# Forming the third expert's weights at half the pace while the filter stage still runs

## The chip, the cores and the metric

One core of one Trainium2 chip runs the kernel. The metric is the device time of one execution in microseconds (us), the median over the timed runs. One further execution was taken with the hardware profiler; all rows in this document come from it.

The core has a matrix engine (PE, with PEld for its weight loads), a vector engine (DVE), a scalar engine (ACT), GpSimd (POOL) and a queue engine that issues DMAs (SP). Each engine works through its own instructions in the order in which the program lists them.

## The reference

The input is a batch of 4 sequences of 3584 rows with 192 columns, 14336 rows in all. Three things are computed one after the other:

```python
# 1: a causal filter of 7 taps per head (8 heads of 24 columns), softmax-normalised taps
out = einsum('hk,bskhg->bshg', softmax(weight), unfold(x_pad))
# 2: a first mixture of 8 experts, one expert per row, with a skip gate and a residual
compute = x @ w_skip > 0
e = argmax(x @ w_gate); g = max(softmax(x @ w_gate))
x[compute] = x + g * (relu(x @ w1[e]) @ w2[e])
# 3: a second mixture of 8 experts, one per row, no residual
e = argmax(x @ w_gate2 + modality_bias[modality_id])
y = g2 * (relu(x @ w1_2[e]) @ w2_2[e])
```

Every expert has w1 of 192 x 1024 and w2 of 1024 x 192 in float32. The kernel multiplies in 16 bits: each operand is split into a high and a low half, and a product is made of three partial products.

## The kernel before

**Filter stage.** `Phase1.run` (lines 970 to 1003) goes through 128 tiles of 112 rows in 8 groups of 16 tiles. A schedule step `v` filters one head of a group, turns earlier rows round and computes gate logits. `Phase1.fin` (line 934) ends a group: it writes each row's expert number, its "code", into `code`, sets `codes = g + 1` and stores the rows in DRAM. `NG` is 8, so `codes == NG` says that all codes are there.

**Routing.** `Moe.route_a` (line 418) turns the codes of a group into positions: a one-hot table `oha`, a running sum on DVE (the scan that writes `cuma`), two small matmuls of `cuma` with `tri` and `ones`, positions `posa`, `sla`, `qa`, comparison tables `oa` and `ob`, and 16 matmuls of `ob` with `oa` that count. After four groups the rows for the first jobs are known; the groups after that are routed beside those jobs.

**Expert weights.** `Moe.prep` (lines 298 to 406) forms the 16-bit weights of the experts one after the other. It loads w1 and w2 into the tiles `ws`, sums their squares for a scale `wsc`, waits for a free buffer (`guard`), and then forms the high halves on ACT (four copies) and the low halves on DVE (eight instructions of the kind "scalar, tensor, tensor": four for w1, 128x512 each, and four for w2, 128x384 each). Between these pieces it yields `p` (lines 372 to 393), so that one piece is issued every `p` schedule steps. `p` is asked for once per expert, when its forming begins:

```python
            p = pace()
            ...
            lo(o1[:, 1, h:], wt[:, h:], sc[:, 0:1], o1[:, 0, h:])
            yield p
```

When an expert is done, `keep` (line 408) stores its formed weights in DRAM. The load of the next expert's tiles is issued between the pieces too, into buffers that the pieces free.

**Jobs.** `Ffn.run` (line 1181) handles blocks of 128 gathered rows, here called jobs, numbered from 0. A job is two halves of `mm1` (20 matmuls `xt,w1b` each), each followed by a high half `hh` on ACT and a low half `hlo` on DVE, and then 24 matmuls `mm2` (`w2b` with `hh` and `hlo`), which come one job later, and the residual sum `x2a` on DVE. Jobs 0 to 2 use the first expert, 3 to 5 the second, 6 to 8 the third, 9 to 11 the fourth. The buffers of `xt` are three; a DMA transposition on SP fills one.

**The order of the work.** Nothing is scheduled by cost. The generators above are advanced by "ticks" (`Tasks.tick`, line 101): the filter loop ticks twice a step, and the job loop ticks once in each of four places of a job (`bg`, line 1469). The last filter steps (from 76 on) and the first two jobs are interleaved. `late()` (line 1342) is true as soon as the third pair of weight buffers exists, which is when the first jobs begin to be prepared. The third expert begins to be formed at filter step 71, in both kernels; at that point six of eight codes exist. `class InOrder` keeps each engine's instructions in the order in which the generators issued them; DMAs on SP are placed by the framework.

Line 73 is the helper that issues every instruction, so it appears in nearly every row; the tiles' names tell the instructions apart. Those that the text speaks of are `w1b` and `w2b` from `ws` and `wsc` (weights being formed), `cuma<-cont,oha` (the scan), `hh`, `hlo`, `x2a`, and `rA`, `rC` (the start of the second routing, `ranks`, line 530, with its own two matmuls on PE).

Of the kernel before, what the change touches and what calls it, by code (L numbers as in the profile page):

```python
# [28 lines left out]
NG = NT // GT  # L29
# [8 lines left out]
LANES = [(0, e) for e in range(E)], [(1, r) for r in range(NSEL)]  # L38
# [1265 lines left out]
def build(tc, x, cw, m1w1, m1w2, mod, bias2, m2w1, m2w2, wgs, out):  # L1304
    with ExitStack() as ctx:
        m = Moe(tc, ctx)
# [9 lines left out]
        pw = ctx.enter_context(tc.tile_pool(name="pw", bufs=2))  # L1316
        pq = ctx.enter_context(tc.tile_pool(name="pq", bufs=4))
# [3 lines left out]
        p1 = Phase1(m, st, sx, x, rows)  # L1321
# [11 lines left out]
        ws = (m1w1, m1w2, s1[0], s2[0]), (m2w1, m2w2, s1[1], s2[1])  # L1333
        d1, d2 = set(), set()
# [7 lines left out]
        owner, conv, late = [None], [False], lambda: len(ffn.w1b) > 2  # L1342

        def lane(k):
            def guard(q, e):
                if q == 0:
                    return e < 2 or late() and (e < 3 or step[0] >= last(e - 3) + 2)
                if "o" in w and owner[0] in (None, k):
                    owner[0] = k
                    return True  # L1350
                return False

            while k and m.sel is None:
                yield 1
            for t in m.prep(ws, w["pw2"] if k else pw, pq, dst, guard, (d1, d2), LANES[k], k, lambda: 8 if k else 8 if late() else 14, lambda: 1 if late() else 3, owner, conv, 8 if k else 26, lambda: not late(), tkw):
                yield t

        def routes():
# [16 lines left out]
        tk, tk2, tkw = Tasks(), Tasks(), Tasks()  # L1375
# [3 lines left out]
        def phase1():  # L1379
            v = next(gp, None)  # L1380
            if v == 1:
                nc.sync.dma_start(rows[0:128, :], m.dz.bitcast(I32))
                nc.sync.dma_start(rows2[0:128, :], m.dz.bitcast(I32))
            if v == 2:
                tkw.add(lane(0))
            if routed[0] < p1.codes:
                tk.add(m.route_a(routed[0], m.code[:, 0, :], rt, ob, ra))
                routed[0] += 1
            return v
# [15 lines left out]
        w = {}  # L1405

        def late_pools():
            st.close()
            m.py.append(m.py2)
            m.ph.append(m.ph3)  # L1410
            px = ctx.enter_context(tc.tile_pool(name="px", bufs=1))
            w["x"] = px.tile([128, NC - XA, D], F32, name="x2s")
            po = ctx.enter_context(tc.tile_pool(name="po", bufs=1))
            pw2 = sp.enter_context(tc.tile_pool(name="pw2", bufs=2))
            w["pw2"] = pw2
            tkw.add(lane(1))
            o = po.tile([128, 4, F], F16, name="o1"), po.tile([128, W2C + 2], F16, name="o2")
            w["o"] = o
            tk.add(routes())
# [174 lines left out]
```

## Time and profile before

| what | value |
|---|---|
| median of 3 timed runs | 985.49 us (984.07 to 986.93) |
| the profiled execution, its own time | 987.25 us |
| span of that execution, first to last instruction | 985.4 us |
| PE busy | 913.1 us, 93% |
| PEld busy | 851.5 us, 86% |
| DVE busy | 589.1 us, 60% |
| ACT busy | 474.5 us, 48% |
| POOL busy | 511.6 us, 52% |
| mean granted clock of PE | 0.968 |

The profiled execution lies 1.76 us above the median, and 1.85 us of its own time lie outside the span. Busy shares are means over stages with different limits; what limits a stage is read from that stage alone. The granted clock is 1 at 2.4 GHz and 0.5 at 1.2 GHz.

### The profile page before, as it was taken

The numbers are of one execution on the slowest core, as the hardware profiler recorded it, in microseconds if no ns is written. First come the engines' busy times: TensorE is split into PE (matmuls) and PEld (weight loads), VectorE is DVE, ScalarE is ACT, GpSimd is POOL, SyncE is SP. The second block draws the span as 40 slices with busy tenths as digits, with TensorE's granted clock in tenths as the row PEclk, the third lists the DMA queues.
The fourth block names the chain that finished last, engine by engine and source line by source line (L and its number), as shares of the span: only waits on it lengthen the run. The fifth ranks groups of instructions, "written<-read, shape, count | busy, mean of one in ns | idle before, by whom it ended". The sixth has DMA issues, their size and how long they took to land. (4 is left out here: it accounts for less than half of the span.)

```text
span 985.4 us, 28847 instructions
## 1 busy us (share of the span) xinstructions
PE 913.1 (93%) x11000; PEld 851.5 (86%) x11000; DVE 589.1 (60%) x1628; ACT 474.5 (48%) x895; POOL 511.6 (52%) x985
## 2 busy tenths in 40 slices
PE   6999859997999999999899999999999999999993
PEld 4676558997999999988888988999989999999992
DVE  5789977899889887446456465864333333333330
ACT  4877743545676655345545654333333333333330
POOL 5055543733547445575667675554555545555431
PEclk9999857999999999999999999999999999999997
DMA  9595576663949685789534334322552332333240
GB/s 320 207 332 188 188 197 192 177 162 71 299 143 262 200 269 149 244 242 344 140 95 109 98 96 114 72 62 65 144 143 72 72 68 75 74 74 74 71 125 15
DMA packets 105910, 148.96 MB, mean 151 GB/s; under 512 B 80559, under 2 KB 85657, under 8 KB 100640
## 3 DMA queue, kind: packets, MB, share of 16 engines
q1 hardware_dynamic: 91136, 117.50, 38.6%
q0 software_dynamic: 13920, 28.87, 12.8%
q8 instruction: 89, 1.46, 0.6%
q14 instruction: 61, 0.50, 0.2%
q10 hardware_dynamic: 704, 0.63, 0.2%
HBM read 174.22 MB, written 51.08 MB: 229 GB/s over the span
## 5 line engine op out<-in xcount | busy, mean ns | idle before, releaser
L73 PEld LDWEIGHTS <-w1b 128*128 128x128 f16 x4200 | 313.8, 99 | 33.5 <-issue 15.8
L73 DVE SCALAR_TENSOR_TENSOR ws<-bank,ws 128x512 f16<-128x512 f32 x220 | 151.3, 690 | 256.3 <-ACT ws L73 212.0
L73 PEld LDWEIGHTS <-ws 128*128 128x128 f16 (+2 forms) x2696 | 224.0, 98 | 2.6
L73 POOL DMA_INDIRECT out_dram<-u,si x114 | 115.6, 1014 | 183.0 <-ACT u L73 72.3
L73 PE MATMUL bank<-xp,w1b 128*128 128x256 f16 x1680 | 201.7, 274 | 4.4 <-DMA xp<-gt 2.7
L73 PE MATMUL bank<-w2b,ws 128*128 128x192 f16 x2016 | 182.8, 247 | 0.0
L73 ACT ACTIVATE ws<-bank 128x512 f16<-128x512 f32 x220 | 130.4, 597 | 94.2 <-PE bank L73 82.6
L73 PE MATMUL bank<-xt,w1b 128*128 128x128 f16 x2520 | 159.0, 223 | 9.2 <-DVE hlo L73 7.5
L73 ACT ACTIVATE hh<-bank 128x512 f16<-128x512 f32 x132 | 78.4, 594 | 143.5 <-PE bank L73 129.8
L73 ACT ACTIVATE u<-bank,c 128x192 f32<-128x192 f32 x114 | 48.0, 421 | 181.3 <-PE bank L73 156.7
L73 PE MATMUL bank<-w2b,hh 128*128 128x192 f16 x1008 | 134.8, 250 | 0.0
L73 PE MATMUL bank<-w2b,hlo 128*128 128x192 f16 x504 | 126.1, 250 | 0.6 <-DVE hlo L73 0.6
L73 DVE SCALAR_TENSOR_TENSOR hlo<-bank,hh 128x512 f16<-128x512 f32 x132 | 90.1, 686 | 53.8 <-ACT hh L73 47.7
L73 PEld LDWEIGHTS <-hh 128*128 128x128 f16 x1056 | 96.1, 100 | 0.6 <-issue 0.3
L73 POOL DMA_INDIRECT gt<-rows,idxm x62 | 62.5, 1009 | 10.5 <-issue 6.2
L73 POOL TENSOR_TENSOR xs<-gt 128x128 f32<-128x128 f16 x124 | 52.5, 445 | 28.1 <-DVE x2a L73 13.0
L73 PEld LDWEIGHTS <-o 128*128 128x128 f16 x640 | 57.0, 98 | 7.0 <-issue 1.6
L73 PE MATMUL bank<-xp,o 128*128 128x256 f16 x520 | 62.0, 273 | 0.3 <-issue 0.3
L73 POOL DMA_INDIRECT gt<-rows,idx x58 | 57.3, 989 | 9.4 <-issue 7.5
L73 PE MATMUL bank<-xg,band 128*112 128x384 f32 x128 | 57.2, 534 | 1.7 <-DVE hl L73 1.7
L73 PE MATMUL bank<-o,ws 128*128 128x192 f16 x624 | 56.4, 247 | 0.0
L73 ACT COPY xtb<-bank 128x672 f16<-128x672 f16 x64 | 45.9, 719 | 18.7 <-PE bank L73 18.4
(301 smaller groups left out, 1257.7 us busy)
## 6 DMA issues: line engine op xcount, KB each, us to landing
w1b<-s1b SPq DMA_DIRECT2D x45, 1024.0 KB
w2b<-s2b SPq DMA_DIRECT2D x45, 768.5 KB
o<-s1b SPq DMA_DIRECT2D x14, 1024.0 KB
o<-s2b SPq DMA_DIRECT2D x14, 768.5 KB
xg<-in_x_dram SPq DMA_DIRECT2D x7, 1536.0 KB
rows<-hl SPq DMA_DIRECT2D x7, 1386.0 KB
ws<-in_moe_w_dram SPq DMA_DIRECT2D x12, 768.0 KB
s1a<-w1b SPq DMA_DIRECT2D x8, 1024.0 KB
```

Of the source, the lines that this page charges most:

```text
L73: r = f(*args, **kw)
```

## The change

The rate of pieces while `late()` holds was 1 for every expert. It becomes 2 as long as a group's codes are missing. The rate is asked for once per expert, and the third expert is the only one that begins while `late()` holds and codes are missing.

```diff
-            for t in m.prep(..., lambda: 8 if k else 8 if late() else 14, lambda: 1 if late() else 3, owner, conv, ...):
+            for t in m.prep(..., lambda: 8 if k else 8 if late() else 14, lambda: (1 if p1.codes == NG else 2) if late() else 3, owner, conv, ...):
```

The third expert's forming begins at filter step 71 in both kernels; it ends in job 0 before, at the end of job 1 now. What follows it in the same generator moves along: the fourth expert's forming runs from the end of job 4 to the end of job 6 before, from the end of job 6 to the end of job 8 now. The scale of the fifth expert is issued two jobs later, and its forming begins at the same place in both kernels. No instruction is added or removed; the lists of PE, DVE and ACT are the same but for their order, POOL's is unchanged.

DVE, in filter steps 73 to 75, where the sixth group is routed (`oa`) and the seventh group's codes are made (`cd` to `code`); `ws_1363` and `ws_1696` are the third expert's w1 and w2:

```order
 L73 SCALAR_TENSOR_TENSOR code<-codeA,code 128x16
-L73 SCALAR_TENSOR_TENSOR w2b_2047<-ws_1696,wsc,w2b_2047 128x2x192
 L73 TENSOR_REDUCE cd<-gec 112x16
 L73 TENSOR_REDUCE gsm<-gex 112x16
 L73 TENSOR_TENSOR oa<-iq,qa 128x1024
-L73 SCALAR_TENSOR_TENSOR w2b_2047<-ws_1696,wsc,w2b_2047 128x2x192
+L73 SCALAR_TENSOR_TENSOR w1b_2046<-ws_1363,wsc,w1b_2046 128x512
 L73 TENSOR_SCALAR gsm<-gsm 112x16
 L73 RECIPROCAL gt<-gsm 112x16
-L73 SCALAR_TENSOR_TENSOR w2b_2047<-ws_1696,wsc,w2b_2047 128x2x192
 L73 TENSOR_TENSOR code<-pm,cd 112x16
 L73 TENSOR_TENSOR code<-cd,code 112x16
```

Three pieces stood here, and one stands here now.

DVE, a little further on, beside job 0, up to the scan of the seventh group (`ws_1572` is the last part of the third expert's w1):

```order
 L73 SCALAR_TENSOR_TENSOR w2b_2047<-ws_1696,wsc,w2b_2047 128x2x192
 L73 TENSOR_REDUCE L<-bank_62 112x68
-L73 SCALAR_TENSOR_TENSOR w1b_2046<-ws_1572,wsc,w1b_2046 128x512
 L73 SCALAR_TENSOR_TENSOR hlo<-bank_58,hh 128x512
 L73 TENSOR_TENSOR oa<-iq,qa 128x1024
 L73 TENSOR_SCALAR pm<-L 112x16
 L73 TENSOR_TENSOR oha<-code,c_144 128x128
-L73 SCALAR_TENSOR_TENSOR w1b_2046<-ws_1572,wsc,w1b_2046 128x512
+L73 SCALAR_TENSOR_TENSOR w2b_2047<-ws_1696,wsc,w2b_2047 128x2x192
 L73 SCALAR_TENSOR_TENSOR cuma<-cont,oha 128x128
```

All eight pieces stood ahead of this scan, and four do now; of the other four, three now stand between it and the eighth group's scan and one behind that.

DVE, at the end of job 8 and the start of job 9 (`bank_58` in the last row is job 9's first half, `ws_2314` the last part of the fourth expert's w1):

```order
 L73 COPY po<-bank_61 128x2x8
 L73 TENSOR_TENSOR off<-po 128x16
 L73 TENSOR_TENSOR off<-off,gend 128x8
+L73 SCALAR_TENSOR_TENSOR w1b_77<-ws_2314,wsc,w1b_77 128x512
 L73 SCALAR_TENSOR_TENSOR x2a<-bank_64,c,xs 128x192
 L73 SCALAR_TENSOR_TENSOR key<-off,c_144 128x8
-L73 TENSOR_TENSOR gt_3236<-key 128x64
-L73 SCALAR_TENSOR_TENSOR hlo<-bank_58,hh 128x512
-L73 TENSOR_REDUCE key<-gt_3236 128x8
+L73 TENSOR_TENSOR gt_3228<-key 128x64
+L73 SCALAR_TENSOR_TENSOR w1b_77<-ws_2314,wsc,w1b_77 128x512
+L73 SCALAR_TENSOR_TENSOR hlo<-bank_58,hh 128x512
```

The fourth expert's eight pieces, which stood from job 5 to job 7, now all stand behind the second scan of `rC`, and the last of them directly ahead of the first `hlo` of job 9, the first job that uses these weights.

## Rows read from the trace of the kernel before

**Rows 1.** Stretches: length; PE, PEld, DVE, ACT, POOL busy; clock; DMA share; GB/s.

```profile
144.35:158.07 13.72, 11.37 (x124) 11.17 (x124) 11.07 (x37) 6.36 (x13) 5.59 (x13) 0.74 0.87 299
158.07:164.25 6.18, 6.18 (x44) 5.93 (x45) 2.06 (x4) 0.00 (x0) 3.27 (x9) 0.52 1.02 201
164.25:193.75 29.50, 28.48 (x410) 28.30 (x408) 25.54 (x64) 12.69 (x19) 16.67 (x38) 0.98 0.49 141
193.75:211.00 17.25, 17.25 (x264) 17.25 (x262) 15.74 (x62) 10.03 (x21) 6.47 (x16) 1.00 0.95 199
211.00:243.80 32.80, 24.72 (x368) 24.01 (x367) 31.70 (x96) 14.11 (x23) 12.76 (x29) 1.00 0.27 64
243.80:250.00 6.20, 6.20 (x71) 6.03 (x70) 6.17 (x13) 2.86 (x4) 1.27 (x4) 0.74 0.94 340
250.00:400.00 150.00, 150.00 (x2166) 150.00 (x2164) 124.88 (x273) 94.32 (x176) 81.97 (x184) 1.00 0.75 218
...
190.09:197.10 7.01, 6.91 (x102) 6.91 (x103) 5.10 (x19) 4.08 (x8) 5.72 (x15) 1.00 1.04 273
```

**Rows 2.** PE in order of time: start us, us, instruction, count, [idle before, releaser].

```profile
144.35 0.59 PE L73 MATMUL bank<-cuma,tri 128*128 128x8 f32 x2 [5.76 <-DVE cuma L73]
...
146.95 4.45 PE L73 MATMUL bank<-xt,w1b 128*128 128x128 f16 x40
...
158.07 0.39 PE L73 MATMUL bank<-cuma,tri 128*128 128x8 f32 x2 [2.35 <-DVE cuma L73]
...
164.25 2.83 PE L73 MATMUL bank<-xt,w1b 128*128 128x128 f16 x40
```

**Rows 3.** DVE in order of time, 133 to 158 us.

```profile
133.37 0.75 DVE L73 SCALAR_TENSOR_TENSOR w1b<-ws,wsc,w1b 128x512 f16<-128x512 f32 x1 [0.57 <-ACT w1b L73]
...
143.88 0.41 DVE L73 TENSOR_TENSOR_SCAN cuma<-cont,oha 128x128 f32<-128x128 f32 x1
...
147.16 0.22 DVE L73 TENSOR_SCALAR t1a<-bank 128x56 f32<-128x56 f32 x1 [0.76 <-PE bank L73]
...
149.92 0.69 DVE L73 SCALAR_TENSOR_TENSOR hlo<-bank,hh 128x512 f16<-128x512 f32 x1 [1.10 <-ACT hh L73]
...
152.06 0.69 DVE L73 SCALAR_TENSOR_TENSOR hlo<-bank,hh 128x512 f16<-128x512 f32 x1 [0.34 <-ACT hh L73]
...
157.38 0.64 DVE L73 TENSOR_TENSOR_SCAN cuma<-cont,oha 128x128 f32<-128x128 f32 x1
```

**Rows 4.** Groups of DVE instructions, 133.3 to 143.95 us: busy us, mean ns, idle.

```profile
L73 DVE SCALAR_TENSOR_TENSOR w1b<-ws,wsc,w1b 128x512 f16<-128x512 f32 x4 | 3.0, 742 | 0.6 <-ACT w1b L73 0.6
L73 DVE SCALAR_TENSOR_TENSOR w2b<-ws,wsc,w2b 128x384 f16<-128x384 f32 x4 | 2.5, 633 | 0.0
```

**Rows 5.** The same groups on DVE, 177.8 to 188.2 us, the fourth expert.

```profile
L73 DVE SCALAR_TENSOR_TENSOR w1b<-ws,wsc,w1b 128x512 f16<-128x512 f32 x4 | 3.4, 848 | 0.0
...
L73 DVE SCALAR_TENSOR_TENSOR w2b<-ws,wsc,w2b 128x384 f16<-128x384 f32 x4 | 2.6, 649 | 0.0
```

**Rows 6.** DVE in order of time: an `hlo` each of jobs 7, 9 and 12.

```profile
188.27 0.68 DVE L73 SCALAR_TENSOR_TENSOR hlo<-bank,hh 128x512 f16<-128x512 f32 x1
...
197.10 0.69 DVE L73 SCALAR_TENSOR_TENSOR hlo<-bank,hh 128x512 f16<-128x512 f32 x1
...
212.99 0.69 DVE L73 SCALAR_TENSOR_TENSOR hlo<-bank,hh 128x512 f16<-128x512 f32 x1
```

**Rows 7.** PE in order of time: the rC matmul, jobs 9, 12, 13 and 18.

```profile
190.19 0.39 PE L73 MATMUL bank<-rC,tri 128*128 128x8 f32 x2 [1.02 <-DVE rC L73]
...
193.75 2.40 PE L73 MATMUL bank<-xt,w1b 128*128 128x128 f16 x40
...
206.78 2.40 PE L73 MATMUL bank<-xt,w1b 128*128 128x128 f16 x40
...
242.49 1.28 PE L73 MATMUL bank<-xt,w1b 128*128 128x128 f16 x20 [3.93 <-DVE hlo L73]
```

**Rows 8.** SP in order of time: the transpositions of jobs 13 and 14.

```profile
203.10 3.16 SPq L1035 DMA_TRANSPOSE xt<-gt  x2
```

More of the change, by code (lines that the diff above doesn't have):

```diff
@@ L1354, in lane @@
                 yield 1
-            for t in m.prep(ws, w["pw2"] if k else pw, pq, dst, guard, (d1, d2), LANES[k], k, lambda: 8 if k else 8 if late() else 14, lambda: 1 if late() else 3, owner, conv, 8 if k else 26, lambda: not late(), tkw):
+            for t in m.prep(ws, w["pw2"] if k else pw, pq, dst, guard, (d1, d2), LANES[k], k, lambda: 8 if k else 8 if late() else 14, lambda: (1 if p1.codes == NG else 2) if late() else 3, owner, conv, 8 if k else 26, lambda: not late(), tkw):
                 yield t
```

## The prediction

> **What bounds the kernel now.** I read the table by stretches first, then the order of time on PE and DVE around the stretches where PE is not busy throughout. From 250 us on, where the last change of order has long passed, PE is busy all of 150 us [rows 1], so whatever the change does earlier is carried to the end as a shift. Ahead of that, three stretches matter. From 144.35 to 158.07 PE is busy 11.4 of 13.7 us and DVE 11.1, at a mean granted clock of 0.74 [rows 1]. PE waits there twice for the scan that writes `cuma`: 5.76 us ahead of 144.35 and 2.35 us ahead of 158.07 [rows 2]. The scan is late because DVE works through its list with hardly a gap, and the third expert's eight pieces are part of that list, 3.0 and 2.5 us busy [rows 4]. The reader should see that DVE sets the pace here, through two scans. From 164.25 to 211.00 PE is full but for one us and DVE has some slack [rows 1]. From 211.00 to 243.80 it turns round: DVE is busy 31.7 of 32.8 us while PE is busy 24.7 [rows 1], and PE's last long wait, 3.93 us for an `hlo` of job 18, ends at 242.49 [rows 7]. So DVE's backlog when it enters that stretch, in jobs 9 to 12, counts one for one.
>
> The change touches both: it relieves DVE ahead of the first scan, and pushes the fourth expert's pieces toward the second backlog.
>
> **Term A, the scans.** Ahead of the first scan stand two w1 and two w2 pieces fewer: 2 x 0.74 + 2 x 0.63 = 2.75 us by their means [rows 4]. Instructions overlap by about 0.08 us each, so 2.4 us of DVE's time. The first piece also waited 0.57 us for its high half on ACT [rows 3]; now the position arithmetic stands ahead of it and covers that. The first scan comes 2.4 + 0.57, about 2.9 us, earlier, and PE's wait of 5.76 shrinks to 2.9 [rows 2]. ACT and POOL follow: the copies that POOL makes from `gt` wait for the same DVE list, and come about 1.5 us earlier.
>
> Between the two scans three pieces are added, two of w2 and one of w1, 2 x 0.55 + 0.66 = 1.8 us without the overlap. DVE waited there 0.76, 1.10 and 0.34 us, 2.2 us in all [rows 3]. Walking down the list with these durations, the whole 0.76 and some 0.4 of the 1.10 are filled; the rest stays, since the high half `hh` comes from PE at the lower clock and is no earlier relative to the scan. So 1.8 - 1.2 = 0.6 us of the 2.9 are given back, and the second scan comes 2.3 us earlier. The eighth piece stands behind it, where DVE waits for PE anyway (busy 2.1 of 6.2 us [rows 1]). Job 3 starts 2.3 us ahead of its 164.25 [rows 2]. Bounds: 1.1 us if none of the waits is filled (2.9 - 1.8), 2.9 if they cover all. I take 2.3, from the walk.
>
> **Term B, the fourth expert.** Its eight pieces, 3.4 + 2.6 = 6.0 us by mean durations [rows 5], 4.8 us at the undisturbed steps of 0.66 and 0.55 (four of each), stood in jobs 5 to 7, where PE is the bound. Taking them away there lets DVE catch up: `hlo` of job 7, which began at 188.27 [rows 6], can begin at about 186.0, when its `hh` is there. The second scan of `rC`, 1.9 us behind that `hlo` to its end, then ends near 187.9 instead of just ahead of 190.19, and PE's wait of 1.02 us for it [rows 7] goes. More than these 2.2 us DVE cannot gain: it waits for `hh`. From there to the second `hlo` of job 9, which began at 197.10 [rows 6], DVE was busy 5.1 of 7.0 us [rows 1]. The eight pieces are added in this piece of the list: 187.9 + 5.1 + 4.8 = 197.8, and some 0.5 us more for the last `hh`, so about 198.4: 1.3 us later than 197.10. PE itself has to wait in job 9, since its weights are finished only then: the last piece but one ends near 194.9, against a start of 193.75 [rows 7] less the 1.02 that went, and the last near 196.5, some 2 us of waiting in place of 1.02. PE gets this back, since from 211 on DVE is what it waits for. So B is +1.3 us. Bounds: 0, if the slack of jobs 9 to 12 takes it, and +4.8, if nothing of the pieces is covered.
>
> **What moves at no cost.** The fifth expert's squares on ACT move by two jobs; ACT is busy 10.0 of 17.25 us there [rows 1], and the forming still waits for the same buffer. On SP, the loads of the fourth expert's w1 and w2 wait longer for the buffers that the pieces free, and what is queued behind them are transpositions whose own buffers become free at about the same time. The tightest is job 12's: it now stands behind the guarded loads of the second mixture's weights, near the place of the transposition that was issued at 203.10 [rows 8], while job 12 begins at 206.78 [rows 7]. The nearest row is that one: 203.10 was early enough for job 13. A lead of under 4 us may leave PE waiting 0 to 3 us, but DVE comes to `hlo` of job 12 only at 212.99 [rows 6], some 4 us behind the `hh`; this is its cover. If DVE had no backlog there, the wait would show. POOL's list does not change.
>
> **The sum.** -2.3 + 1.3 = -1.0 us. From the profiled execution's 987.25 us that gives 986.2; that execution lies 1.76 us above the median of the runs, so on the median it is 985.49 - 1.0 = 984.5 us. Smaller than the 0.3%, 3.0 us, that a measurement of this kernel can tell from no change. The own range of this case is 983.0 to 986.0.
>
> **The rivals.**
>
> *The clock stays up (981.8 us).* After the 5.76 us of idling PE ran job 1 at the lower level: 4.45 us for 40 matmuls [rows 2], against 2.40 in job 9 [rows 7]. The stretch ahead of job 3 has a clock of 0.52, and there are two dozen matmuls of `mm2` in it [rows 1]. With waits of 2.9 us or less PE might keep 2.4 GHz. Job 1 would be 2.05 us shorter, of which DVE, with its own list, passes on about 0.7; the stretch of 6.18 us ahead of job 3, without the counting matmuls some 4 us, would lose about 2. That is 2.7 us more: 984.5 - 2.7 = 981.8. Against it speaks that 2.35 us of idling ahead of 158.07 was enough to lead into the 0.52, and that gaps of that size remain.
> The Trainium skill, "TensorE: Matmul & The Clock Gate", Part 1, says that the throttled level is the default and activity releases it, and that the observation runs freely, so that the moment varies from run to run. By that rule a shorter pause could leave the clock up, and the time would be this rival's. The trace agrees that the level falls after a pause, at 0.74 and 0.52; whether a pause half as long suffices, no row shows.
>
> *The fourth expert is late (988.4 us, slower).* If DVE does not catch up in jobs 5 to 7, because `hh`, `x2a` and the `rC` scans have their own inputs to wait for, all 4.8 us of its pieces land behind 197.10, and A is no better than -2.3: 985.49 + 2.5 = 988.0. A PE wait of 4 us in job 9 would also bring the lower clock, as the one of 3.93 us did (0.74 from 243.80 to 250.00 [rows 1]); what of that DVE does not hide I put at 0.4 us. The point from which it decides is B = 2.3: then nothing is gained. For it speaks that the last piece stands directly ahead of job 9's `hlo`; against it that DVE's `hlo` of job 7 is 2 us behind its input, which is slack to be caught up.
>
> *The gain ends at job 3 (986.8 us).* A transposition or a gather that SP and POOL hold up could keep job 3 and the next ones at their old place; then A is 0 and B stays: 985.49 + 1.3. For it speaks that SP now waits for the third expert's last pieces ahead of job 4's and job 5's transpositions; against it that each of these jobs lies more than 10 us behind.
>
> That the change does nothing at all is excluded by the order of the instructions.
>
> **How the numbers follow.** The forecast has a chance of 0.55, the clock 0.15, the late fourth expert 0.15, the lost gain 0.15. Faster by over 0.3% (under 982.5) needs the clock rival, in over half of its chance, or the upper ends of A and of B: 0.09 + 0.08 = 0.17. Slower (over 988.4) needs the late expert, in over half of its chance, or the lost gain with more than 1.3 in B: 0.09 + 0.03 = 0.12. Within: 0.71. The range from 981.7 to 988.0 takes in the forecast, the lost gain and about half of each of the other two; it leaves out some 0.1 below and 0.1 above.
>
> **What would show it.** Right: PE's first wait for `cuma` falls from 5.76 to about 2.9 us and the second stays near 2.4; job 3 starts near 162; PE's wait for `rC` is gone; PE waits about 2 us for `w1b` in job 9; the second `hlo` of job 9 begins near 196 (198.4 less the 2.3); the wait that ended at 242.49 ends near 241.5. Wrong: job 3 at 164 or later refutes A, matmuls of job 1 at 2.4 GHz bring the clock rival, and a second `hlo` of job 9 behind 197.5 brings the late expert.

## The result, and the profile after

The change is slower: 994.45 us (median of 6 runs, 992.28 to 997.70) against 986.45 us of the kernel before on the same chip, a ratio of 1.0075 with a 95% interval from 1.0056 to 1.0093. The prediction was 984.5 us, range 981.7 to 988.0, and gave "slower" a chance of 0.12. The profiled execution took 994.03 us (span 992.2, clock 0.966); that of the kernel before 987.25 (985.4, 0.968).

One thing ahead of the comparison: two profiles do not start alike. Ahead of the first instruction that the change moves on DVE, the profile after already lies 1.25 us behind (DVE reduces `L<-bank` at 129.20 before and at 130.45 after). Job 0's first product starts at 134.69 (before) and 135.75 us (after), and in the twelve profiles of this case anywhere from 134.26 to 137.65. So a position that says "counted from job 0" has the start of job 0's first product of its own profile taken off; the other positions are those of the profile as it stands.

PE of the changed kernel in order of time (start us, us, instruction, count, idle before and its releaser):

```profile
142.71 0.60 PE L73 MATMUL bank<-cuma,tri 128*128 128x8 f32 x2 [3.03 <-DVE cuma L73]
...
145.33 4.25 PE L73 MATMUL bank<-xt,w1b 128*128 128x128 f16 x40
...
156.93 0.59 PE L73 MATMUL bank<-cuma,tri 128*128 128x8 f32 x2 [3.14 <-DVE cuma L73]
...
163.32 3.82 PE L73 MATMUL bank<-xt,w1b 128*128 128x128 f16 x40
...
192.76 0.39 PE L73 MATMUL bank<-xt,w1b 128*128 128x128 f16 x4
196.16 3.54 PE L73 MATMUL bank<-xt,w1b 128*128 128x128 f16 x36 [3.02 <-DVE w1b L73]
201.93 2.40 PE L73 MATMUL bank<-xt,w1b 128*128 128x128 f16 x40
206.15 2.40 PE L73 MATMUL bank<-xt,w1b 128*128 128x128 f16 x40
214.19 3.95 PE L73 MATMUL bank<-xt,w1b 128*128 128x128 f16 x40 [3.67 <-DMA xt<-gt]
220.35 2.40 PE L73 MATMUL bank<-xt,w1b 128*128 128x128 f16 x40
...
247.77 1.92 PE L73 MATMUL bank<-xt,w1b 128*128 128x128 f16 x20 [3.93 <-DVE hlo L73]
```

Against [rows 2] the first wait for `cuma` has fallen from 5.76 to 3.03 us, the second has grown from 2.35 to 3.14 (the scan is earlier, but PE is still earlier). Against [rows 7] there are two new waits: 3.02 us for the fourth expert's `w1b` in job 9, and 3.67 us for the transposition of job 12. Behind the first, 36 products take 3.54 us, and behind the second, 40 take 3.95, where 40 take 2.40 in the undisturbed jobs. The granted clock shows why: 0.70 and 0.73 of 2.4 GHz in these two stretches (next fence, last column but two).

```profile
196.16:201.93 5.77, 5.69 (x60) 5.38 (x61) 4.48 (x15) 2.23 (x4) 2.44 (x5) 0.70 0.94 290
214.19:220.35 6.16, 6.16 (x68) 6.16 (x68) 4.99 (x8) 2.73 (x5) 2.88 (x5) 0.73 0.68 216
```

DVE of the changed kernel in order of time (the last piece of the fourth expert, the second `hlo` of job 9, the choice of experts for the second mixture, the first `hlo` of job 12):

```profile
196.94 0.81 DVE L73 SCALAR_TENSOR_TENSOR w1b<-ws,wsc,w1b 128x512 f16<-128x512 f32 x1
...
200.37 0.69 DVE L73 SCALAR_TENSOR_TENSOR hlo<-bank,hh 128x512 f16<-128x512 f32 x1 [0.84 <-ACT hh L73]
...
201.48 0.17 DVE L73 TENSOR_SCALAR sel<-key 128x8 int32<-128x8 f32 x1
...
217.15 0.69 DVE L73 SCALAR_TENSOR_TENSOR hlo<-bank,hh 128x512 f16<-128x512 f32 x1 [1.11 <-ACT hh L73]
```

SP of the changed kernel in order of time. The guarded loads fetch the second mixture's weights of the expert that `sel` names, so they read `sel` and cannot issue before it is written, at 201.48; the three transpositions (jobs 12 to 14) stand behind them:

```profile
203.19 0.36 SPq L310 DMA_DIRECT2D ws<-in_moe_w_dram  x1
204.36 1.22 SPq L317 DMA_DIRECT2D ws<-in_moe_w_dram  x2
206.37 0.36 SPq L322 DMA_DIRECT2D ws<-in_moe_w_dram  x1
206.84 4.21 SPq L1035 DMA_TRANSPOSE xt<-gt  x3
```

**Where the time went.** From the start of job 9 to the second half of job 18, which waits 3.93 us for `hlo` in both kernels, the kernel before needs 242.49 - 193.75 = 48.74 us [rows 7], the changed one 247.77 - 192.76 = 55.01. The difference of 6.27, taken from the starts of the first products of the jobs (a positive number is a loss):

| jobs | change | what |
|---|---|---|
| 9 | +4.95 | wait for `w1b` 3.02, lower clock 1.9 |
| 10 | -0.38 | the product for the fifth expert's sums of squares is no longer here |
| 11 (up to job 12's start) | +3.83 | wait for the transposition 3.67 |
| 12 | +1.94 | lower clock 1.55, and that product |
| 13, 15, 17 | -1.61, -1.03, -1.43 | PE's waits for `hlo` are gone |
| 14, 16, 18 | 0 | |

The waits that are gone are these, of the kernel before (PE in order of time):

```profile
213.73 1.28 PE L73 MATMUL bank<-xt,w1b 128*128 128x128 f16 x20 [1.46 <-DVE hlo L73]
223.60 1.28 PE L73 MATMUL bank<-xt,w1b 128*128 128x128 f16 x20 [0.87 <-DVE hlo L73]
233.40 1.28 PE L73 MATMUL bank<-xt,w1b 128*128 128x128 f16 x20 [1.21 <-DVE hlo L73]
```

So PE gives up 10.7 us and gets 4.5 back. Ahead of job 9 the change had gained 0.99 us, and 6.27 - 0.99 = 5.28 us is how late the wait of 3.93 us ends. Counted from job 0 the gain ahead of job 9 is 2.05 us (59.06 - 57.01) and the lateness 4.22; the other 1.06 lay there when job 0 began. The 5.28 stay to 400 us and beyond. Some 1.5 us more come in the later stages of the profile, and the medians differ by 8.0; this remainder wasn't traced.

### The profile page after: what moved, and what is told of

Its sections match the earlier page's. It is cut to its first block, busy times and chain, and to the rows that moved or that the text cites. A ratio compares the mean times of both kernels' runs of the same rounds, so it can differ in the third digit from the quotient of the medians.

```text
span 992.2 us, 28848 instructions
## 1 busy us (share of the span) xinstructions
PE 917.7 (92%) x11000; PEld 854.6 (86%) x11000; DVE 589.1 (59%) x1628; ACT 475.5 (48%) x895; POOL 512.7 (52%) x985
## 5 line engine op out<-in xcount | busy, mean ns | idle before, releaser
L73 PE MATMUL bank<-xt,w1b 128*128 128x128 f16 x2520 | 161.5, 225 | 12.0 <-DMA xt<-gt 4.9
```

What stands on the lines that cost most here:

```text
L73: r = f(*args, **kw)
```

## The experiments

The theory after the result: the third expert's slower pace is a small gain; the loss has two parts, the fourth expert's late pieces (job 9) and job 12's transposition behind the guarded loads. The rival: the slower pace itself costs, since PE idles in other places and runs at the lower clock. Each run is compared with the kernel before on its own chip. Its median was 977.4 us beside the first four runs below, 985.3 beside the two that say "of 985.27", and 978.6 beside the others; so ratios are compared, and microseconds only within one chip.

**The fourth expert back near its old place**, with the slower pace kept:

```diff
-                    yield 2 if k < 3 else 5
+                    yield (1 if k < 3 else 4) if n == 3 and lane == 0 else 2 if k < 3 else 5
...
-                    yield 4 + 12 * q
+                    yield 1 if n == 2 and lane == 0 else 4 + 12 * q
```

> The change, but the fourth expert's forming is started two schedule steps earlier again (close to its place in the kernel before; the transposition of job 12 is then again ahead of the guarded loads of the second mixture). Theory (the fourth expert came late and that made job 12's transposition late; the slower pace of the third expert by itself is a small gain): PE has no wait above 1.5 us for w1b in job 9 and none above 1 us for xt in job 12, the second hlo of job 9 begins near 196 to 197, time 984 to 987 against 986.45 of the kernel before. Rival (the slower pace itself costs, through the lower clock in job 3 and what follows): time 991 to 995, as with the change.

Measured: ratio 0.9996 (0.9974 to 1.0018), 977.72 us. No wait for `w1b` and none for job 12's transposition; the second `hlo` of job 9 begins at 195.45. The whole loss is gone with the fourth expert's delay, so the rival falls. But no gain is left to measure in the time either, within the 2.2 us of the interval. The profile does show one: counted from job 0, `hlo` of job 20 begins at 119.25, against 121.90 in the profile of the kernel before. Of these 2.65 us, some 1.3 are that one profile's own: its job 3 starts at 29.56, and at 28.20 to 28.27 in the three other runs at the old pace without fillers.

**The fourth expert late alone**, third at its old pace:

```diff
-                    yield 4 + 12 * q
+                    yield 12 if n == 2 and lane == 0 else 4 + 12 * q
```

> The kernel before, third expert at its old pace, but the fourth expert's forming started eight ticks later, at the schedule step where the change has it; job 12's transposition then stands behind the guarded loads, as with the change. Theory: all the loss is here, and no gain of the scans: PE waits 2 to 4 us for w1b in job 9 and 3 to 4 us for xt in job 12, time 993 to 997. Rival (the slower pace itself costs): 985 to 988.

Measured: 1.0091 (1.0058 to 1.0123), 986.49 us: as slow as the change, without its slower pace. The second wait is larger than expected:

```profile
193.62 3.81 PE L73 MATMUL bank<-xt,w1b 128*128 128x128 f16 x36 [2.47 <-DVE w1b L73]
...
213.71 4.32 PE L73 MATMUL bank<-xt,w1b 128*128 128x128 f16 x40 [5.87 <-DMA xt<-gt]
```

**The change with job 12's transposition ahead of the guarded loads.** The second mixture's generator (`lane(1)`, so `k` is 1) begins four ticks later and waits four ticks less afterwards (its first pause, 8, becomes 4, in a line not shown):

```diff
             while k and m.sel is None:
                 yield 1
+            for _ in range(4 * k):
+                yield 1
```

> The change, but the second mixture's guarded loads begin four ticks later (and their squares at the same tick as before), so that SP issues job 12's transposition ahead of them; nothing else differs in PE's or DVE's order up to job 12. Theory (two waits in a row, for w1b in job 9 and for the transposition in job 12): the first stays at about 3 us, the second, 3.67 us, falls under 1 us, the first product of job 12 takes 2.4 us in place of 3.95, time 989 to 991. Rival (the late fourth expert alone; DVE's list would have been as late without the transposition): 993 to 995.

Measured: 1.0032 (1.0013 to 1.0051), 980.06 us. PE and SP in order of time:

```profile
193.64 1.29 PE L73 MATMUL bank<-xt,w1b 128*128 128x128 f16 x20 [2.46 <-DVE w1b L73]
195.29 1.89 PE L73 MATMUL bank<-xt,w1b 128*128 128x128 f16 x16 [0.35 <-DVE w1b L73]
...
208.19 2.40 PE L73 MATMUL bank<-xt,w1b 128*128 128x128 f16 x40
```

```profile
197.21 1.75 SPq L1035 DMA_TRANSPOSE xt<-gt  x1
200.74 0.37 SPq L310 DMA_DIRECT2D ws<-in_moe_w_dram  x1
```

The transposition is issued at 197.21, job 12 starts at 208.19 without a wait, and its product takes 2.40 us. The wait for `w1b` stays. About half of the loss was the queue: 0.43% of the 0.75%, or 0.28% of the 0.60% when the change is measured again below. These are runs on different chips, and the intervals of this run and of that second measurement overlap; the pair that follows stands on one chip.

**Both at the old pace: fourth expert late, transposition ahead** (the two edits above on the kernel before):

> As the run with the fourth expert late alone (third at its old pace), and the guarded loads four ticks later, so that job 12's transposition stands ahead of them. Theory: only the wait for w1b is left, time 988.5 to 991, some 3 to 5 us less than with the transposition behind. Rival (the late expert alone is the whole loss): 993 to 997, the same as with it behind.

Measured: 1.0041 (1.0021 to 1.0060), 981.29 us; the wait for `w1b` is 2.47, that for job 12's transposition is gone. Between it and the run with the transposition behind (982.32 to 990.35 us in single runs, here 977.97 to 984.87) lie 0.50%, 4.9 us. PE still waits 0.62 us for the transposition of job 13.

**The fourth expert one schedule step late**, third at its old pace (8 in place of the 12 above):

> The kernel before, third expert at its old pace, the fourth expert's forming one schedule step later than there (the change has it two steps later); job 12's transposition is still ahead of the guarded loads. Theory (what decides is whether the last w1 piece is ready when job 9 wants it; one step is about 4.2 us, and two steps make PE wait 2.5 to 3.0 us): no wait for w1b in job 9 above 0.5 us, time as the kernel before within 1.5 us. Rival (each step of delay pushes DVE's pieces into the second backlog, so the cost grows in proportion): half of the 4.0 us of the run with two steps and the transposition ahead, +2 us.

Measured: 1.0032 (1.0013 to 1.0051), 982.50 us. The expectation held an error of mine: in this kernel too the transposition stands behind the guarded loads. So PE meets the queue without the late weights:

```profile
202.04 2.39 PE L73 MATMUL bank<-xt,w1b 128*128 128x128 f16 x40
211.75 4.33 PE L73 MATMUL bank<-xt,w1b 128*128 128x128 f16 x40 [4.95 <-DMA xt<-gt]
```

```profile
199.97 0.37 SPq L310 DMA_DIRECT2D ws<-in_moe_w_dram  x1
...
204.32 3.87 SPq L1035 DMA_TRANSPOSE xt<-gt  x3
```

PE doesn't wait for `w1b`, as the theory said, and the time is lost at job 12: counted from job 0, `hlo` of job 11 begins 1.0 us earlier than in the kernel before, that of job 14 and all later ones up to job 55 1.3 to 1.8 us later. That is 2.3 to 2.8 us, on a wait of 4.95: DVE's backlog gives the rest back. Neither theory's number was right, for that reason.

**The change once more:**

> The change once more, beside the other runs. Theory: ratio 1.006 to 1.009; a wait of 2.4 to 3.1 us for w1b in job 9 and 3 to 4 us for xt in job 12; relative to the first product of job 0 the first cuma scan is 2.9 us and the second 2.3 us earlier than in the kernel before.

Measured: 1.0060 (1.0038 to 1.0083), 984.12 us; waits of 2.46 and 0.35 us for `w1b` and 3.95 for the transposition. The scans come 2.8 and 2.5 us earlier, counted from job 0 (6.84 and 20.87 against 9.66 and 23.38).

**Why the earlier scans bring so little: the clock.** In all four profiles with the slower pace and no filler (the change twice, the transposition ahead, the fourth expert back) job 3's first product takes 3.82, 3.97, 3.82 and 3.78 us; in the four at the old pace 2.83, 2.71, 2.80 and 2.69. PE reaches the second scan earlier than its data, waits over 3 us, and runs on at the lower clock. To test it, PE got something to do in that wait, on top of the fourth expert back near its place. `g` is the group whose scan is waited for, counted from 0, and `fill` a piece of a result bank that takes products nobody reads:

```diff
+        self.fill = bk[3][:, 256:384]
...
         pp = self.misca
+        for _ in range({7: 48}.get(g, 0)):
+            nc.tensor.matmul(self.fill, self.ident, self.ident, start=True, stop=True)
```

> As the run with the fourth expert back near its place, and 48 products of the identity with itself (128 columns, result unused) on PE directly ahead of the product that waits for the second cuma scan. Theory (the gain of the scans is real, 2.3 us at job 3, and about half of it is lost because PE, after its wait of about 3.5 us, runs mm2 and the first product of job 3 at the lower clock): with the wait filled the clock stays at 2.4 GHz, the first product of job 3 takes 2.4 to 2.8 us in place of 3.78, job 4 starts 1 to 2 us earlier than without the filler, time 975.5 to 977.5 where the kernel before has 977.4. Rival (what follows job 3 is paced by DVE and the scans, not by the clock): job 3's product is shorter but job 6 starts no earlier, time as without the filler, ratio 1.000.

Measured: 0.9938 (0.9913 to 0.9963), 972.33 us of 978.61. PE in order of time:

```profile
153.60 2.84 PE L73 MATMUL bank<-ident 128*128 128x128 f16 x48
156.90 0.39 PE L73 MATMUL bank<-cuma,tri 128*128 128x8 f32 x2 [0.46 <-DVE cuma L73]
157.14 0.37 PE L73 MATMUL bank<-cuma,ones 128*128 128x8 f32 x2
161.08 2.40 PE L73 MATMUL bank<-xt,w1b 128*128 128x128 f16 x40
165.69 2.39 PE L73 MATMUL bank<-xt,w1b 128*128 128x128 f16 x40
```

Job 4 starts 30.10 us after job 0's product; without the filler it was 32.10 (167.81 - 135.71). Job 6 starts 2.0 us earlier too (40.27 against 42.28), so the rival falls. The gain in the time is larger than expected: the ratio is 0.58% below that of the run without the filler (taken on another chip), 5.7 us, and of these the profile shows 2.0 up to `hlo` of job 20 (117.27 against 119.25). Where the rest comes from wasn't traced. Once more, beside the kernel before with fillers of its own:

> The slower pace of the third expert, the fourth expert back near its place and the filler at the second scan, once more beside the kernel before with fillers. Theory: ratio 0.993 to 0.997, 1.5 to 2.5 us below the kernel before with fillers. Rival (the slower pace is worth nothing): the two kernels within 0.5 us of each other.

Measured: 0.9952 (0.9932 to 0.9972), 980.00 us of 985.27: faster than the kernel before a second time. The stretch from the second scan's product to job 3, without the filler (fourth expert back) and with it:

```profile
156.59:161.82 5.23, 5.23 (x45) 5.11 (x46) 2.60 (x5) 0.47 (x2) 3.75 (x9) 0.62 0.97 344
```

```profile
158.70:162.89 4.19, 4.19 (x44) 4.19 (x45) 2.59 (x5) 0.81 (x2) 3.75 (x9) 1.00 1.05 431
```

The same work takes 5.23 us at a granted clock of 0.62 and 4.19 at 1.00.

**The kernel before with fillers**, 40 and 36 products (`{6: 40, 7: 36}` in the line above):

> The kernel before, third expert at its old pace, with products of the identity on PE ahead of the two products that wait for the cuma scans: 40 at the first (where PE waited 5.76 us), 36 at the second (2.35 us). It tells whether the slower pace is worth anything once PE's clock is held up. Theory (the clock and the scans each have their own price: holding the clock saves about 2 us, the slower pace another 2.3 us at job 3): job 3 starts near 26.8 to 27.3 us after the first product of job 0, against 29.56 in the kernel before and 25.5 with pace and filler together; ratio 0.997 to 0.999. Rival (the filler alone is the whole gain, the slower pace is worth nothing): ratio as with pace and filler together, 0.994 to 0.996.

Measured: 0.9990 (0.9969 to 1.0012), 984.10 us of 985.27. Job 3 starts 27.70 us after job 0's product, a little behind what was expected, and 0.5 us ahead of the 28.2 of the other runs at the old pace. Fillers put into the kernel before don't bring the gain. The run above is 0.38% below it, 3.7 us, more than the 1.5 to 2.5 expected. But the two runs don't separate the pace from the clock: these fillers did not hold it (job 1's product takes 3.90 us, job 3's 2.90). What the old pace would gain with the clock held, no run shows.

**Fillers at both scans**, slower pace, fourth expert back (`{6: 20, 7: 48}`):

> As the run with the filler at the second scan, and 20 more such products ahead of the one that waits for the first cuma scan. Theory of the clock: job 1 too runs at 2.4 GHz, its first product near 2.4 us in place of 3.8; DVE is the bound between the scans, so at most 0.5 us more, time 975 to 977. Rival: the second scan comes no earlier and the time is that of the filler at the second scan alone, or of none.

Measured: 0.9969 (0.9949 to 0.9990), 974.57 us. Job 1's product falls to 2.42 us, but PE then waits 1.52 us for an `hlo` of DVE, and the second scan comes 20.59 us after job 0's product, 0.3 us earlier than without any filler: between the scans DVE is the bound, so this part adds nothing that can be told.

## Why the prediction was wrong, step by step

**Term A was right in its place and was then half lost.** The first scan was to come 2.9 us earlier, the second and job 3 2.3. Counted from job 0 it was 2.7, 2.2 and 2.0 in the two first profiles, and 3.1, 2.4 and 2.25 by the means over the four profiles at each pace (job 3 at 28.57 and 26.32). What failed was to let job 3's start stand for the gain. I priced only a clock that stays up more; job 3's product at 3.8 instead of 2.8 us was not in the sum. The rival by which the clock stays up fell with it: after a wait of 3.03 us job 1's product took 4.25. By `hlo` of job 6 the means over the same profiles stand at 45.8 and 44.7: 1.2 us are left of A.

**Term B was mis-sized: about +3.2 in place of +1.3.** The walk down DVE's list held: the `rC` wait is gone, and the last piece, which was to end near 196.5 less the 2.3 of A, 59.5 counted from job 0, released PE at 59.85 in the second profile of the change; in the first, where job 6 already starts 1.45 us later than in the second, it ended at 62.0. The wait of some 2 us was 2.5 to 3.0. Missing were the 1.9 us that PE loses behind it at the lower clock, although [rows 1] and [rows 2] had shown twice that PE works at this level behind a wait, and the late-expert rival named it with 0.4 us. With the transposition ahead, the profiles give from job 6 to job 20 +3.3 (slower pace) and +3.1 (old pace).

**"What moves at no cost" was the step that decided.** The prediction saw that job 12's transposition would stand behind the guarded loads, put PE's wait at 0 to 3 us, and wrote it off against DVE's lateness of 4 us at job 12's `hlo`. The lead of under 4 us was read rightly: 3.7 us (issued at 206.84, wanted at 210.52). Two things were wrong. First, the bound of the wait: the one row it was judged by, job 13's issue at 203.10 for a start at 211.00, only says that 7.9 us were enough there, and 7.9 - 3.7 = 4.2, not 3. Measured from issue to product are 7.35 and 8.28 us in the two profiles of the change, 7.43 and 9.35 in the runs with the fourth expert late at the old pace, so even 7.9 was no safe bound. Second, again, the clock behind the wait: 1.5 us. So the cover had to hide not 0 to 3 us but 3.67 + 1.55 = 5.2 in the first profile of the change, and 5.87 + 1.90 = 7.8 at the old pace.

The cover itself was there. With the transposition ahead, `hlo` of job 12 begins 5.61 us behind the start of job 12 on PE (208.19), in the kernel before 6.21 [rows 6, 7], so the late pieces had hardly touched it (DVE of that run):

```profile
213.80 0.68 DVE L73 SCALAR_TENSOR_TENSOR hlo<-bank,hh 128x512 f16<-128x512 f32 x1
```

From job 6 to job 20 the profiles with the transposition behind are 1.9 and 2.3 us later than with it ahead for the change, and 4.2 at the old pace. So the cover hid some 3.3 to 3.5 us, near the 4 forecast; part of what it could not hide shows as DVE's wait of 1.11 us for `hh` at that `hlo`, where DVE does not wait in the kernel before [rows 6]. Between the transposition behind and ahead, the ratios differ by 0.28 and 0.43% for the change (its two measurements) and by 0.50% at the old pace: 2.8 to 4.9 us.

The Trainium skill, "Perfetto Trace Analysis", section "Per-instruction lifecycle: what the profiler-reported window actually captures", says that for a DMA the whole movement of data lies outside the window that the profile shows. The rows here agree: 4.21 us of issue for three transpositions, and 7.35 us until the first one's data is used.

**The sum** was -2.3 + 1.3 + 0 = -1.0. In the profiles it is about -1.2 + 3.2 + 1.9 to 4.2, some +4 to +6 us; the medians give +8.0, and the second measurement of the change, 0.60% of 986.45, gives +5.9. The difference stays open. The rival "the fourth expert is late", at 988.4, had the right sign and named the late expert. Its reason, that DVE does not catch up, did not hold, since the wait for `rC` is gone; and its price lacked the queue and had 0.4 us for the clock.

**The signs on record** had told the cases apart: the first wait for `cuma` was 3.03 (about 2.9 said) and job 3 started at 163.32, so A was not refuted; job 1 stayed at the lower clock; and the second `hlo` of job 9 behind 197.5 was to mean the late expert. It began at 200.37.

## What to carry to other kernels

A cover is a difference of two times, and both belong to the kernel after the edit: set against it all that the covered engine's input loses, the wait and the slower work behind the wait together. When a step moves behind one that reads a register or waits for a computed value, everything behind it on that issuing queue moves too; price a transfer from issue to use, by a row where it was just late, not by one where it was early enough. And when an edit opens or moves a wait of PE, price the products behind it at the lower clock; a wait that can't be removed may be worth filling.

## What the hardware showed that was not expected

Products without a use, in a wait of PE, made the kernel faster: 48 of them, 2.84 us, held the granted clock at 1.00 and gave back a microsecond in the 4 us behind them and 1.4 us in job 3's product. The time fell by 0.4 to 0.6% against the run without them, of which the profiles up to job 20 show 2.0 and 2.2 us. They don't always do it: in the kernel before with fillers, 40 products took 2.69 us at a granted clock of 0.89, PE then waited 2.79 us, and job 1's product still took 3.90. With 20 products and a wait of 1.61 it took 2.42.
